# Attention softmax: the division by the row sums moved from the probabilities to the output of the product with V

## The chip, the core and the metric

One core of a Trainium2 chip runs the whole program. The metric is device time in microseconds of one execution; shorter is better. The engines are TensorE (PE, with its weight loads listed as PEld), VectorE (DVE), ScalarE (ACT), GpSimd (POOL), and the queue SP, which here issues all DMA transfers. Each engine works through its own queue in order.

## The reference

The program computes an attention block and two feed-forward blocks. Only the first part is touched here:

```python
B, H, S, D = q.shape                       # 4, 8, 576, 64
scores = scale * np.matmul(q, k.transpose(0, 1, 3, 2))
scores = np.where(causal, -1000000000.0, scores)
scores = scores - scores.max(-1, keepdims=True)
a = np.exp(scores)
a /= a.sum(-1, keepdims=True) + 1e-09
local = np.matmul(a, v)
...
return (g * mem_out + (1 - g) * local).astype(np.float32)
```

The result has 2304 tokens by 512 columns. It goes through `a*b @ w3 @ w_out` with `a = x @ w1`, `b = x @ w2`, and then through `(h - tanh h) @ w_out` with `h = x @ w_in`.

## The kernel before

The 32 heads are handled as 16 pairs P (two heads of one batch), and the 576 queries of a pair as five units u: u = 0 to 3 are 128 queries of each head, and u = 4 is the last 64 queries of both heads, stacked on 128 partitions. There are so 80 units. For each unit, `scores` makes the masked scores in PSUM (tile `sc`), `rmax` takes the negative row maximum on DVE into the small tile `st`, `exps` writes the exponentials to the tile `p` on ACT and lets the instruction add up the row sums into columns 2 and 3 of `st`, and `norm` makes the reciprocal of these sums on DVE (L416, L418, L420) and multiplies `p` by it on POOL, one instruction for each head (L427). `trans` turns `p` on PE, 128 by 128 blocks at a time, into the PSUM tile `t`, and `copy` brings `t` to the SBUF tiles `g`. `av` multiplies V with `g`, for units 0 and 1 as one group (256 queries) and for units 2 to 4 as another (320 queries), into the PSUM tile `o`, whose 128 partitions are the 64 columns of the two heads, and whose columns are the queries. The last step of `av` copies `o` to the tiles `xs`, scaled by `omgt`, which is 1 - g per partition.

`copy` shares its work: four of each five calls go to ACT (L438), the fifth to DVE (L440 or, with a scale, L442), counted over all its calls.

The loop over the units runs the steps in the order of `ORDER`, each with a lag:

```python
ORDER = "SENTLGA"
LAG = {'S': 0, 'E': 0, 'N': 0, 'T': 1, 'L': 0, 'G': 3, 'A': 2}
...
for m in range(NU + 8):
    for x in ORDER:
        do(x, m - LAG[x])
```

So `norm` of a unit stands one turn ahead of its `trans`, and `trans` one turn ahead of `av`. The letter L is one step of `prep_qk` for the next pair: it splits q and k in two parts each, on ACT, POOL and DVE (L204, L208, L219, L224, L226), and at its end issues the load of the pair after (`r`, one buffer). The letter G runs some steps of background work: decoding of the weights (L74 to L99, on ACT, DVE and POOL), the product of w3 and w_out (PSUM tile `fo`, which shares its two buffers with `o`), and the memory term. The order in each engine's queue isn't that of the program text: the framework simulates a timeline with its own costs and sorts the instructions by it, within their dependences (`schedule_with_timeline_sim=True`).

The PSUM pools are `pss` with four buffers (`sc`), `psT` with two (`t`) and `psA` with two (`o`). After the attention, phase B makes the first feed-forward block and phase C the second.

Of the kernel before, what the change touches and what calls it, by code (L numbers as in the profile page):

```python
# [11 lines left out]
F32 = mybir.dt.float32  # L12
F32R = mybir.dt.float32r
BF16 = mybir.dt.bfloat16
U32 = mybir.dt.uint32
U16 = mybir.dt.uint16
I64 = mybir.dt.int64
AF = mybir.ActivationFunctionType
# [6 lines left out]

# (h - tanh h) / h^3 as a product of two squares plus constants in u = h^2, for u <= TANH_SPLIT^2
TANH_SPLIT = 0.6
# [5 lines left out]
def block_kernel(ctx, tc, qk, qt, vt, mp, zp_d, beta, w1, w2, w3t, wo, wi, wo2, ident_d, mask_d, out):  # L33
# [11 lines left out]

# [1 line left out]
    ident = cp.tile([128, 128], F32, name="ident")  # L47
# [11 lines left out]

# [1 line left out]
    def dec_load(src):  # L61
# [39 lines left out]
    class Decoder:  # L101
        """Decodes a list of (source, destination) in turn, some at a time, with its loads ahead."""

# [38 lines left out]
    def mm(o, lhsT, rhs, start, stop):  # L142
        return PE.matmul(o, lhsT, rhs, start=start, stop=stop).ins  # L143
# [31 lines left out]
    CPA = (0, 1, 3, 4)  # L175
# [1 line left out]
    att = ExitStack()  # L177
# [9 lines left out]
    KH, KL = [[[t[:, x, h] for h in range(2)] for t in KF] for x in range(2)]  # L187
    V = [ap1.tile([128, 5, 2, 64], F32, name=f"v{i}") for i in range(2)]

    raw_t = {}  # L190
# [41 lines left out]

# [1 line left out]
    WF = {}  # L234
# [66 lines left out]
    if True:  # L301
# [23 lines left out]
        for i in range(2):  # L325
            PO.memset(QF[i][:, 0:64].bitcast(U32), 0)
            PO.memset(QF[i][:, 1216:1280].bitcast(U32), 0)
        xs = {}

# [11 lines left out]

# [1 line left out]
        pst = ExitStack()  # L343
# [40 lines left out]
        def rmax(n, x):  # L384
# [11 lines left out]
            if u == 4 and x == 1:  # L396
                DV.tensor_tensor(out=st_t[n][:, 0:1], in0=st_t[n][:, 0:1], in1=st_t[n][:, 1:2], op=ALU.min)

        def exps(n, x):
            P, u = units[n]  # L400
            st = st_t[n]
            if x == 0:
                p_t[n] = ap3.tile([128, PW[u]], F32, tag=f"p{u}" if PU else "p", name="p")
            w = width(u, x)
            o = x * (w if u < 4 else 320)
            b = x if u < 4 else 0
            mark["A"][n] = AC.activation(out=p_t[n][:, o:o + w], in_=sc_t.pop((n, x))[:, 0:w], func=AF.Exp,  # L407
                                         bias=st[:, b:b + 1], accum_out=st[:, 2 + x:3 + x]).ins

        def norm(n):  # L410
            P, u = units[n]
            hp = P % 4
            st, p = st_t.pop(n), p_t[n]
            w = 2 if u < 4 else 1
            if u < 4:
                DV.tensor_scalar(out=st[:, 4:6], in0=st[:, 2:4], scalar1=1e-9, scalar2=None, op0=ALU.add)  # L416
            else:
                DV.scalar_tensor_tensor(out=st[:, 4:5], in0=st[:, 2:3], scalar=1e-9, in1=st[:, 3:4],  # L418
                                        op0=ALU.add, op1=ALU.add)
            DV.reciprocal(out=st[:, 6:6 + w], in_=st[:, 4:4 + w])  # L420
            K = 128 * (u + 1) if u < 4 else 576
            for h in range(w):
                pr, sc = p[:, K * h:K * h + K], st[:, 6 + h:7 + h]
                if NV[u] == "A" or NV[u] == "H" and h or NV[u] == "Q" and P % 2:
                    AC.activation(out=pr, in_=pr, func=AF.Copy, scale=sc)
                else:
                    (DV if NV[u] == "V" else PO).tensor_scalar(out=pr, in0=pr, scalar1=sc, scalar2=1.0, op0=ALU.mult, op1=ALU.mult)  # L427

# [15 lines left out]
        def trans(n):  # L444
            P, u = units[n]
            p = p_t.pop(n)
            if u == 0:
                g_t[0] = ap2.tile([128, 2, 2, 256], F32, tag="g0", name="g0")
            if u == 2:
                g_t[1] = (ap1, ap2)[G1 - 1].tile([128, 4, 2, 320], F32, tag="g1", name="g1")  # L450
                g_t[2] = ap2.tile([64, 2, 64], F32, tag="g2", name="g2")
            if u < 4:
                K = 128 * u + 128
                blocks = [(kb, h) for kb in range(u + 1) for h in range(2)]
                for c in range(0, len(blocks), 4):
                    ch = blocks[c:c + 4]
                    t = psT.tile([128, 4, 128], F32, tag="t", name="t")
                    for m, (kb, h) in enumerate(ch):
                        PE.transpose(t[:, m], p[:, K * h + 128 * kb:K * h + 128 * kb + 128], ident)  # L459
                    G = g_t[0] if u < 2 else g_t[1]  # L460
                    q0 = 128 * (u % 2)
                    copy(G[:].rearrange("p a b q -> p (a b) q")[:, c:c + len(ch), q0:q0 + 128], t[:, 0:len(ch)])
            else:
                t = psT.tile([128, 4, 128], F32, tag="t", name="t")
                for kb in range(4):
                    PE.transpose(t[:, kb], p[:, 128 * kb:128 * kb + 128], ident)
                copy(g_t[1][:].rearrange("p a b q -> p (a b) q")[:, :, 256:320],
                     t[:].rearrange("p a (b q) -> p (a b) q", b=2))
                t = psT.tile([128, 4, 128], F32, tag="t", name="t")
                PE.transpose(t[0:64, 0], p[:, 512:576], ident)  # L470
                copy(g_t[2][:], t[0:64, 0].rearrange("p (b q) -> p b q", b=2))

        finished = [0]

        def av(P, grp):
# [5 lines left out]
            if grp == 0:  # L481
                for kb in range(2):
                    for h, r in hr:
                        mm(o[r, 128 * kb:256], v[:, kb, h], g_t[0][:, kb, h, 128 * kb:256], kb == 0, kb == 1)
            else:
                for kb in range(4):
                    q0 = 128 if kb == 3 else 0
                    for h, r in hr:
                        mm(o[r, q0:320], v[:, kb, h], g_t[1][:, kb, h, q0:320], kb == 0, False)
                for h, r in hr:  # L490
                    mm(o[r, 256:320], v[0:64, 4, h], g_t[2][:, h], False, True)
            ch = b * 9 + grp * 4
            finished[0] = 2 * P + grp + 1
            for X, e0, e1, s in xpart(ch, ch + n // 64):
                copy(X[:, e0:e1, hp], o[:, 64 * s:64 * (s + e1 - e0)].rearrange("p (a b) -> p a b", b=64),
                     omgt[:, hp:hp + 1])

# [1 line left out]
        N = 384  # L499
# [139 lines left out]
        def do(x, n):  # L639
# [15 lines left out]
            elif x == "T":  # L655
                trans(n)
            elif x == "A" and u in (1, 4):
                av(P, u // 4)
# [26 lines left out]

# [1 line left out]
        pools = {}  # L687
# [169 lines left out]

# [1 line left out]
        c2 = ctx.enter_context(tc.tile_pool(name="c2", bufs=2))  # L859
# [180 lines left out]
```

## Time and profile before

| | |
|---|---|
| median of 3 runs | 1068.35 us (1066.63 to 1069.19) |
| span of the profiled execution | 1064.0 us |
| mean granted TensorE clock | 0.973 |
| PE busy | 991.2 us, 93% of the span |
| DVE busy | 824.1 us, 77% |
| ACT busy | 609.3 us, 57% |
| POOL busy | 439.8 us, 41% |

The span runs from the first to the last instruction of the profiled execution. Its own time isn't listed apart from that; the median of the runs is 4.35 us above the span. Busy time is the union of an engine's instructions. Matmuls are pipelined, so that PE can be called busy while it could still take more work. The product with V of the last pair, the end of the attention, stands at some 305 us; phase B and C follow.

### The profile page before, as it was taken

To read this page: it belongs to the slowest core of one execution; us is meant where nothing else is said; L and a number is where in the kernel's file an instruction comes from. 1 tells how busy PE (TensorE), PEld (TensorE's weight loads), DVE (VectorE), ACT (ScalarE), POOL (GpSimd) and SP (SyncE) were. 2 spreads that over 40 slices of the span, in tenths; PEclk is the share of its full clock that TensorE was granted. 3 is DMA by queue.
4 is the path that set the end of the run, shared out by engine and by line. 5 is a ranking of instruction groups with operands and counts; after the bars stand their busy time and mean duration, and the time that the engine had idled before them with its cause. 6 is when DMAs were issued, how large, how long until landed. Compare 5 with 4: busy or idle time off the path is not lost.

```text
span 1064.0 us, 15807 instructions
## 1 busy us (share of the span) xinstructions
PE 991.2 (93%) x5512; PEld 863.2 (81%) x5512; DVE 824.1 (77%) x1465; ACT 609.3 (57%) x1413; POOL 439.8 (41%) x446
## 2 busy tenths in 40 slices
PE   5889898976999899999999997999999999999998
PEld 3566666654688798999999987789999999999997
DVE  7999999999869985557221498988878787787875
ACT  5767677666832332324121444678777776776864
POOL 5788677777655432200000485532222222222221
PEclk8899999999999999999999998999999999999999
DMA  7665575554324451123100013000000000000000
GB/s 199 162 161 153 165 190 132 140 136 124 94 74 131 157 155 60 50 70 130 50 1 1 20 60 99 20 1 30 1 1 30 1 30 1 1 31 2 30 1 30
DMA packets 44415, 77.73 MB, mean 73 GB/s; under 512 B 5168, under 2 KB 30000, under 8 KB 42416
## 3 DMA queue, kind: packets, MB, share of 16 engines
q1 hardware_dynamic: 44336, 76.73, 25.3%
q8 instruction: 43, 0.70, 0.3%
q14 instruction: 36, 0.29, 0.1%
HBM read 72.00 MB, written 4.72 MB: 72 GB/s over the span
## 4 chain that ended last, share of the span: by engine, by line
PE 61%; DVE 18%; DMA 8%; POOL 6%; issue 4%; ACT 2%; SPq 0%; DVEq 0%; POOLq 0%; ACTq 0%
PE o L143 20%; PE h L143 18%; PE ab L143 13%; PE x L143 6%; DMA r<-in_qk 6%; DVE T L81 2%; DVE T L75 2%; DVE T L84 2%; POOL p L427 1%; DMA raw<-in_wo 1%; DVE T L77 1%; DVE qs L224 1%; PE mo L143 1%; DVE st L394 1%; PE t L459 1%
## 5 line engine op out<-in xcount | busy, mean ns | idle before, releaser
L922 POOL TENSOR_TENSOR gl<-s,gh 128x384 fp32r<-128x384 f32 x96 | 102.2, 1065 | 285.2 <-ACT gh L916 266.8
L427 POOL TENSOR_SCALAR p<-p,st 128x128 f32<-128x128 f32 (+2 forms) x144 | 111.4, 787 | 45.0 <-DVE st L420 25.3
L143 PE MATMUL ab<-xh,wa 128*128 128x384 f32 x384 | 110.1, 344 | 4.9 <-DVE a L723 1.9
L143 PE MATMUL x<-abh,wf 128*128 128x384 f32 x384 | 109.3, 346 | 3.2 <-ACT abh L726 3.2
L143 PE MATMUL ab<-xh,wb 128*128 128x384 f32 x384 | 108.3, 340 | 3.5 <-POOL wb L96 3.1
L143 PE MATMUL sc<-ks,qs 128*128 128x256 f32 (+4 forms) x384 | 91.3, 355 | 14.4 <-DVE qs L224 8.8
L898 DVE SCALAR_TENSOR_TENSOR s<-s,u 128x384 f32<-128x384 f32 x96 | 82.6, 860 | 24.3 <-ACT s L888 23.5
L407 ACT ACTIVATE p<-sc,st 128x256 f32<-128x256 f32 (+4 forms) x160 | 82.6, 524 | 28.4 <-DVE st L391 11.7
L74 ACT ACTIVATE T<-raw 128x512 f32<-128x512 f32 x72 | 48.5, 674 | 86.8 <-DMA raw<-in_wo 29.0
L723 DVE TENSOR_TENSOR a<-ab,a 128x384 f32<-128x384 f32 x48 | 26.5, 552 | 81.2 <-PE ab L143 68.5
L894 ACT ACTIVATE u<-u,pc 128x384 f32<-128x384 f32 x96 | 59.3, 619 | 43.9 <-DVE s L898 43.8
L143 PEld LDWEIGHTS ab<-xh,wa 128*128 128x128 f32 x384 | 71.1, 190 | 9.7 <-issue 3.3
L143 PEld LDWEIGHTS sc<-ks,qs 128*128 128x128 f32 x384 | 62.2, 203 | 20.3 <-ACT ks L204 7.5
L143 PEld LDWEIGHTS x<-abh,wf 128*128 128x128 f32 x384 | 71.9, 192 | 4.4 <-ACT abh L726 4.1
L904 DVE TENSOR_TENSOR t<-h,t 128x384 f32<-128x384 f32 x96 | 53.2, 554 | 28.5 <-ACT t L887 28.0
L143 PEld LDWEIGHTS ab<-xh,wb 128*128 128x128 f32 x384 | 71.0, 190 | 4.8 <-POOL wb L96 3.8
L459 PE MATMUL t<-ident,p 128*128 128x128 f32 x320 | 53.0, 286 | 20.2 <-ACT g L438 8.1
L903 DVE SCALAR_TENSOR_TENSOR s<-s,s 128x384 f32<-128x384 f32 x96 | 65.5, 682 | 7.9
L143 PE MATMUL x<-abl,wf 128*128 128x384 f32 x192 | 66.3, 345 | 3.8 <-DVE abl L727 3.7
L886 ACT ACTIVATE u<-h 128x384 f32<-128x384 f32 x96 | 46.9, 488 | 39.8 <-PE h L143 39.8
L143 PE MATMUL h<-xh,wf 128*128 128x384 f32 x240 | 67.7, 343 | 1.0 <-DVE s L905 1.0
L143 PE MATMUL h<-xh,z 128*128 128x384 f32 x240 | 66.7, 338 | 0.8 <-DVE s L905 0.8
(205 smaller groups left out, 2811.9 us busy)
## 6 DMA issues: line engine op xcount, KB each, us to landing
r<-in_qk SPq DMA_DIRECT2D x30, 576.0 KB, 6.7
raw<-in_wo SPq DMA_DIRECT2D x24, 512.0 KB, 3.5
raw<-in_w3t SPq DMA_DIRECT2D x16, 512.0 KB, 4.6
raw<-in_w SPq DMA_DIRECT2D x16, 512.0 KB, 3.6
raw<-in_wi SPq DMA_DIRECT2D x16, 512.0 KB, 3.7
v<-in_vt SPq DMA_DIRECT2D x16, 320.0 KB, 5.1
mw<-in_qt SPq DMA_DIRECT2D x18, 256.0 KB, 3.0
out<-ob SPq DMA_DIRECT2D x18, 256.0 KB, 2.3
```

What stands on the lines that cost most here:

```text
L74: AC.activation(out=tf, in_=hw.bitcast(F32), func=AF.Abs)
L143: return PE.matmul(o, lhsT, rhs, start=start, stop=stop).ins
L407: mark["A"][n] = AC.activation(out=p_t[n][:, o:o + w], in_=sc_t.pop((n, x))[:, 0:w], func=AF.Exp, bias=st[:, b:b + 1], accum_out=st[:, 2 + ...
L427: (DV if NV[u] == "V" else PO).tensor_scalar(out=pr, in0=pr, scalar1=sc, scalar2=1.0, op0=ALU.mult, op1=ALU.mult)
L459: PE.transpose(t[:, m], p[:, K * h + 128 * kb:K * h + 128 * kb + 128], ident)
L723: DV.tensor_tensor(out=a, in0=o[1][:, 0:N], in1=a, op=ALU.mult)
L886: AC.activation(out=u, in_=o, func=AF.Square)
L894: AC.activation(out=u, in_=u, func=AF.Relu, bias=pc[:, 2:3])
L898: DV.scalar_tensor_tensor(out=s1, in0=s1, scalar=k2[0], in1=u, op0=ALU.add, op1=ALU.mult)
L903: DV.scalar_tensor_tensor(out=s1, in0=s2, scalar=k2[1], in1=s1, op0=ALU.add, op1=ALU.mult)
L904: DV.tensor_tensor(out=t, in0=o, in1=t, op=ALU.subtract)
L922: PO.tensor_tensor(out=l, in0=s1, in1=h[:].bitcast(F32), op=ALU.subtract)
```

## The change

`exps` lets the sums of all units of a group go to one tile `sg`. `norm` does nothing for units 0, 2 and 3; at units 1 and 4, the last of their groups, it adds 1e-9 and takes the reciprocals of the whole group at once on DVE, and lets POOL spread the first four columns of them into a tile `rb` of 128 by 256, each column 64 times. The tile `p` isn't multiplied any more: `trans` reads what `exps` wrote. A new step `spread`, behind `trans` of the same unit, turns `rb` on PE with two transposes, and for the second group a fifth column with a third, into a tile of the pool `psT`; ACT then copies this to a tile `rr` and multiplies by `omgt` on the way, in one instruction for the first group and in three for the second. The last step of `av` is now a DVE multiplication of `o` by `rr`, instead of the copy with a scale; it doesn't count any more for the share-out in `copy`. The tile `g2`, of 64 partitions before, has 128, whose upper half is set to zero at the start; the last two matmuls of a group multiply with all 128 rows of it.

```diff
+    G2 = [ap1.tile([128, 2, 64], F32, name=f"g2{i}") for i in range(2)]
...
+            PO.memset(G2[i][64:128].bitcast(U32), 0)
...
+        sum_t, rr_t, inv_t = {}, {}, {}
+
         def exps(n, x):
             P, u = units[n]
             st = st_t[n]
+            grp, a = (0, 2 * u) if u < 2 else (1, 2 * u - 4)
+            if u in (0, 2) and x == 0:
+                sum_t[P, grp] = ap4.tile([128, 16], F32, tag="sg", name="sg")
+            sg = sum_t[P, grp]
...
-                                         bias=st[:, b:b + 1], accum_out=st[:, 2 + x:3 + x]).ins
+                                         bias=st[:, b:b + 1], accum_out=sg[:, a + x:a + x + 1]).ins
 
         def norm(n):
             P, u = units[n]
-            hp = P % 4
-            st, p = st_t.pop(n), p_t[n]
-            w = 2 if u < 4 else 1
-            if u < 4:
-                DV.tensor_scalar(out=st[:, 4:6], in0=st[:, 2:4], scalar1=1e-9, scalar2=None, op0=ALU.add)
-            else:
-                DV.scalar_tensor_tensor(out=st[:, 4:5], in0=st[:, 2:3], scalar=1e-9, in1=st[:, 3:4],
+            st_t.pop(n)
+            if u not in (1, 4):
+                return
+            grp = u // 4
+            sg = sum_t.pop((P, grp))
+            DV.tensor_scalar(out=sg[:, 8:12], in0=sg[:, 0:4], scalar1=1e-9, scalar2=None, op0=ALU.add)
+            if grp:
+                DV.scalar_tensor_tensor(out=sg[:, 12:13], in0=sg[:, 4:5], scalar=1e-9, in1=sg[:, 5:6],
                                         op0=ALU.add, op1=ALU.add)
-            DV.reciprocal(out=st[:, 6:6 + w], in_=st[:, 4:4 + w])
-            K = 128 * (u + 1) if u < 4 else 576
-            for h in range(w):
-                pr, sc = p[:, K * h:K * h + K], st[:, 6 + h:7 + h]
-                if NV[u] == "A" or NV[u] == "H" and h or NV[u] == "Q" and P % 2:
-                    AC.activation(out=pr, in_=pr, func=AF.Copy, scale=sc)
-                else:
-                    (DV if NV[u] == "V" else PO).tensor_scalar(out=pr, in0=pr, scalar1=sc, scalar2=1.0, op0=ALU.mult, op1=ALU.mult)
+            w = 13 if grp else 12
+            DV.reciprocal(out=sg[:, 8:w], in_=sg[:, 8:w])
+            rb = ap2.tile([128, 256], F32, tag="rb", name="rb")
+            PO.tensor_scalar(out=rb[:].rearrange("p (a b) -> p a b", b=64),
+                             in0=sg[:, 8:12].unsqueeze(2).to_broadcast([128, 4, 64]),
+                             scalar1=1.0, scalar2=1.0, op0=ALU.mult, op1=ALU.mult)
+            inv_t[P, grp] = sg, rb
+
+        def spread(n):
+            P, u = units[n]
+            if u not in (1, 4):
+                return
+            grp, hp = u // 4, P % 4
+            sg, rb = inv_t.pop((P, grp))
+            t = psT.tile([128, 4, 128], F32, tag="t", name="rt")
+            for m in range(2):
+                PE.transpose(t[:, m], rb[:, 128 * m:128 * m + 128], ident)
+            if grp:
+                PE.transpose(t[:, 2], sg[:, 12:13].to_broadcast([128, 128]), ident)
+            r = rr_t[P, grp] = ap2.tile([128, 320], F32, tag="rr", name="rr")
+            o = omgt[:, hp:hp + 1]
+            AC.activation(out=r[:, 0:256], in_=t[:, 0:2].rearrange("p a b -> p (a b)"), func=AF.Copy, scale=o)
+            if grp:
+                for h in range(2):
+                    x = slice(64 * h, 64 * h + 64)
+                    AC.activation(out=r[x, 256:320], in_=t[x, 2, x], func=AF.Copy, scale=o[x])
...
-                g_t[2] = ap2.tile([64, 2, 64], F32, tag="g2", name="g2")
+                g_t[2] = G2[P % 2]
...
-                copy(g_t[2][:], t[0:64, 0].rearrange("p (b q) -> p b q", b=2))
+                copy(g_t[2][0:64], t[0:64, 0].rearrange("p (b q) -> p b q", b=2))
...
-                    mm(o[r, 256:320], v[0:64, 4, h], g_t[2][:, h], False, True)
+                    mm(o[r, 256:320], v[:, 4, h], g_t[2][:, h], False, True)
...
+            rr = rr_t.pop((P, grp))
             for X, e0, e1, s in xpart(ch, ch + n // 64):
-                copy(X[:, e0:e1, hp], o[:, 64 * s:64 * (s + e1 - e0)].rearrange("p (a b) -> p a b", b=64),
-                     omgt[:, hp:hp + 1])
+                c = slice(64 * s, 64 * (s + e1 - e0))
+                DV.tensor_tensor(out=X[:, e0:e1, hp], in0=o[:, c].rearrange("p (a b) -> p a b", b=64),
+                                 in1=rr[:, c].rearrange("p (a b) -> p a b", b=64), op=ALU.mult)
...
                 trans(n)
+                spread(n)
```

## Rows read from the trace of the kernel before

**Rows 1.** Busy time in stretches: start:end, length, then each engine, clock, DMA.
```profile
0.00:100.00 100.00, 79.06 (x447) 56.71 (x447) 88.49 (x171) 64.89 (x177) 75.14 (x90) 0.90 0.66 170
100.00:250.00 150.00, 129.32 (x847) 94.40 (x849) 143.82 (x286) 100.24 (x284) 111.34 (x124) 0.97 0.57 151
250.00:305.00 55.00, 49.02 (x342) 33.83 (x339) 43.80 (x110) 36.19 (x103) 34.57 (x43) 0.97 0.31 88
305.00:450.00 145.00, 134.12 (x766) 123.14 (x765) 114.03 (x215) 49.52 (x105) 57.14 (x48) 0.96 0.36 111
```

**Rows 2.** Waits, DVE, 0 to 305 us: total us, times, longest.
```profile
DVE ks L226 <- POOL ks L208: 4.2, 6, 1.7
...
DVE g L440 <- PE t L466: 1.3, 1, 1.3
```

**Rows 3.** Groups by line, DVE, 0 to 305 us: busy, mean ns, idle before.
```profile
L224 DVE SCALAR_TENSOR_TENSOR qs<-r,qs 64x576 fp32r<-64x576 f32 x32 | 31.3, 990 | 7.5 <-ACT qs L219 6.6
...
L226 DVE TENSOR_TENSOR ks<-r,ks 128x576 fp32r<-128x576 f32 x16 | 21.7, 1353 | 4.2 <-POOL ks L208 4.2
L416 DVE TENSOR_SCALAR st<-st 128x2 f32<-128x2 f32 x64 | 19.6, 307 | 0.1
L75 DVE TENSOR_SCALAR T<-T 128x512 f32<-128x512 f32 x30 | 19.1, 636 | 3.2 <-ACT T L74 2.8
L77 DVE TENSOR_SCALAR T<-T 128x512 uint32<-128x512 uint32 x30 | 18.6, 619 | 0.2
L440 DVE COPY g<-t 128x512 f32<-128x512 f32 (+2 forms) x29 | 17.6, 609 | 1.3 <-PE t L466 1.3
...
L420 DVE RECIPROCAL st<-st 128x2 f32<-128x2 f32 (+1 forms) x80 | 11.9, 155 | 0.3
L418 DVE SCALAR_TENSOR_TENSOR st<-st 128x1 f32<-128x1 f32 x16 | 10.9, 682 | 1.1 <-ACT p L407 1.1
...
L587 DVE TENSOR_TENSOR xs<-mo,xs 128x384 f32<-128x384 f32 x4 | 2.2, 554 | 0.4 <-PE mo L143 0.4
```

**Rows 4.** Instructions of tile xs, 0 to 305 us: shortest/median/longest ns, first and last start.
```profile
L442 DVE TENSOR_SCALAR xs<-o,omgt x4: 339/440/539, 43.7 to 267.6; 128x192 f32<-128x192 f32 x1, 128x128 f32<-128x128 f32 x1, 128x256 f32<-128x256 f32 x1, 128x320 f32<-128x320 f32 x1
```

**Rows 5.** Groups by line, POOL, 0 to 305 us.
```profile
L427 POOL TENSOR_SCALAR p<-p,st 128x128 f32<-128x128 f32 (+2 forms) x144 | 111.4, 787 | 45.0 <-DVE st L420 25.3 <-DVE st L416 9.9 <-PE sc L143 3.0
...
L99 POOL TENSOR_TENSOR zs<-T,zs 128x512 fp32r<-128x512 f32 x16 | 22.4, 1400 | 1.3
```

**Rows 6.** Groups by line and shape, POOL, 0 to 305 us.
```profile
L427 POOL TENSOR_SCALAR p<-p,st 128x256 f32<-128x256 f32 x32 | 21.4, 680 | 12.1 <-DVE st L416 7.1 <-PE sc L143 3.0 <-DVE st L420 1.5
```

**Rows 7.** Instructions of four DVE lines, 0 to 305 us: shortest/median/longest ns.
```profile
L75 DVE TENSOR_SCALAR T<-T x30: 409/430/1516, 13.3 to 265.6; 128x512 f32<-128x512 f32 x30
...
L77 DVE TENSOR_SCALAR T<-T x30: 405/427/1422, 14.2 to 268.8; 128x512 uint32<-128x512 uint32 x30
...
L224 DVE SCALAR_TENSOR_TENSOR qs<-r,qs x32: 749/783/1880, 6.6 to 264.6; 64x576 fp32r<-64x576 f32 x32
...
L226 DVE TENSOR_TENSOR ks<-r,ks x16: 745/1332/1986, 7.4 to 260.4; 128x576 fp32r<-128x576 f32 x16
```

**Rows 8.** Timeline: start, length, engine, line, count: eight transposes in a row.
```profile
197.65 1.04 PE L459 MATMUL t<-ident,p 128*128 128x128 f32 x8
```

**Rows 9.** Waits, PE, 0 to 305 us: total us, times, longest.
```profile
PE t L459 <- ACT g L438: 8.1, 8, 3.0
PE fo L143 <- POOL zs L96: 7.9, 5, 2.4
PE t L459 <- DVE g L440: 6.4, 8, 1.5
...
PE t L459 <- POOL p L427: 4.6, 3, 2.3
```

**Rows 10.** Groups by line and shape, ACT, 0 to 305 us.
```profile
L219 ACT ACTIVATE qs<-r 128x576 fp32r<-128x576 f32 x32 | 21.0, 680 | 16.3 <-DMA r<-in_qk 16.3
...
L438 ACT ACTIVATE g<-t 128x256 f32<-128x256 f32 x29 | 11.2, 386 | 5.4 <-PE t L459 5.4
...
L438 ACT ACTIVATE xs<-o,omgt 128x256 f32<-128x256 f32 x15 | 7.1, 472 | 2.0 <-PE o L143 2.0
...
L438 ACT ACTIVATE g<-t 64x128 f32<-64x128 f32 x13 | 3.4, 260 | 0.3 <-PE t L470 0.3
```

## The prediction

> **What bounds the kernel now.** I began with busy time in stretches [rows 1]. The attention ends at some 305 us, and everything that the change touches lies ahead of that. In its middle, 100 to 250 us, DVE is busy for 143.8 of 150 us (96%), PE for 129.3, ACT for 100.2, POOL for 111.3. So DVE sets the pace there. At both ends it is less clear: in the other 155 us of the attention DVE is busy for 88.5 + 43.8 = 132.3, or 85%. Over all 305 us the sums are DVE 276.1, PE 257.4 and POOL 221.1. What comes behind 305 us is untouched, and there PE is busy for 134.1 of the first 145 us: a shorter attention starts that part earlier, and changes nothing in it.
>
> The second view is who waits for whom. DVE hardly waits: 4.2 us for POOL's part of k, 1.3 us in all for transposed blocks, though it fetches some thirty of them from PE [rows 2]. PE waits more: 14.5 us in 16 pieces for `t` to be emptied, 7.9 us for weights that POOL splits and 4.6 us for the scaled `p` [rows 9]. ACT's largest single wait is 16.3 us for the load of q and k [rows 10].
>
> The third view is the duration of one DVE instruction. Lines whose operands all lie in SBUF scatter: L75 takes 409 ns at the shortest and 636 in the mean, L77 405 and 619, L224 749 and 990, L226 745 and 1353 [rows 3, 7]. The multiplication L587, with one input in PSUM, is at 554 [rows 3]. So something in SBUF holds DVE up, and POOL, busy for 72% of this stretch, is the engine that I hold it to be. Half of POOL's time is L427, 111.4 of 221.1 us [rows 1, 5], and just this goes.
>
> **DVE's own work.** Removed: 64 additions at 307 ns (19.6 us), 16 of L418 at 682 (10.9), 80 reciprocals at 155 (12.4) [rows 3], and four copies to `xs` at 440 (1.8) [rows 4]: 44.7 us. Added: with one set for each of 32 groups, 32 additions (9.8), 16 of L418 (10.9), 32 reciprocals (5.0), all at the same durations, since widths of 1 to 5 columns differ in nothing that counts. Then the multiplications of `o` by `rr`. There are 36: 16 of 256 columns, 12 of 320, and 4 pairs whose group is cut at token block 6, in 128 and 192. The copies L442 do the same move in 339 ns at 128 columns and 539 at 320, thus 1.04 ns a column [rows 4]; by them the 36 cost 17.0 us. L587 takes 554 for 384 columns with two inputs of the same kinds [rows 3]; with the same slope 256 cost 421, 320 cost 487, and the 36 cost 15.1. I take 15.1, the same operation, and keep 17.0 as the upper end. Added are 40.8 us, 3.9 less than removed. Since these steps leave the count in `copy`, a fifth of 138 calls (128 of `t`, 10 of the memory term) stays with DVE, about 28; now it has 29 and one more that isn't shown; two fewer at 609 are 1.2 us [rows 3]. DVE's own work falls by 5.1 us.
>
> **What POOL gives back to DVE.** The four scattering lines lose 30 x 227 + 30 x 214 + 32 x 241 + 16 x 608 ns = 30.6 us against their shortest [rows 3, 7]. POOL loses 111.4 us of L427 and gains 32 spreads of 256 columns; nearest is L427 at that width, 680 ns, so 21.8 us [rows 5, 6]. POOL's time falls by 89.6 of 221.1 us, 40%, and 40% of 30.6 is 12.2 us. The bounds are 0 (if POOL's longer instructions, L99 at 1400 ns and its like, do the holding [rows 5]) and 27 (if nearly all of it is L427, which stands close behind DVE's small steps). L427 is short at 787 ns in the mean, which speaks for less than its share; L81, L84 and L397, of the same kind and left out of the sum, for more. I stay at 12.2. DVE in all: -17.3 us.
>
> A rule of the Trainium skill (SBUF — State Buffer, Who interferes with whom) says that GpSimd and a VectorE instruction with two SBUF inputs, or in a mode that uses both ports, exclude each other for a whole instruction, the later one being blocked fully. By that rule every overlap that goes is time for one of the two, and the gain would lie near the upper bound; no row here divides the blocked time between them.
>
> **PE.** It gets 2 transposes for each of 32 groups and a third for 16: 80. Eight in a row take 1.04 us [rows 8], so at most 0.13 us each, 10.4 us in all. PE's 257.4 us become 268, while DVE's 276.1 become 259. PE would pass DVE if its shown time were full; it is not, since matmuls overlap and the shown time holds the tail of each run. I cost the 10.4 us at nothing, under DVE's work, and let only half of the gain pass where DVE isn't full; uncovered they are 10 us. The last two matmuls of a group multiply 128 rows in place of 64, with the same columns: nothing, under the same cover, as is the zeroing at the start, on an idle POOL.
>
> On this point the Trainium skill (TensorE: Matmul & The Clock Gate, Part 4: PE-mode transpose) speaks against the change: it gives a transpose some 275 ns in a kernel, which as a cost would be an estimated 22 us for the 80. The trace doesn't agree to that as a cost, since eight take 1.04 us, 0.13 each [rows 8].
>
> **ACT and the waits.** ACT loses 32 copies to `xs` of about 472 ns (15 us) and gains 32 of 256 columns at 386 (12.4) and 32 of 64 by 64, at most 260 each (8.3) [rows 10]: up 6 us, on an engine with 104 us free (305 less 201 busy, [rows 1]); nothing. No DMA is moved; the loads of `r` are set free by L224 and L226, which come sooner if DVE is quicker. POOL's spread waits for DVE's reciprocal, with POOL's splits behind it; PE's transposes of `rb` wait for it, with the next scores behind them. Both stand a turn ahead of the product with V, and the multiplication by `rr` is the only wait at the end. There DVE waits for `o`, with the row maxima and so the exponentials behind it. By the 1.3 us over 29 copies [rows 2, 3] that is 0.045 us each, 1.6 us for 36.
>
> **Sum.** From 100 to 250 us DVE is at 96%, so its share of the gain passes through: 17.3 x 150/305 = 8.5 us. In the remainder, with DVE at 85% and the load of `r` waited for [rows 1, 10], I let half pass: 4.4. Less 1.6 for the new wait makes 11.3 us. The span goes from 1064.0 to 1052.7; the median stands 4.35 us above the span, so 1068.35 becomes 1057.0.
>
> **Rivals.** *POOL was the real brake.* L427 also holds the splits that PE waits for (7.9 us) and `p` itself (4.6) [rows 9], and the DVE steps that stay could fall toward their undisturbed length. With 27 us of relief, DVE's work falls by 32; with the waits on POOL gone too, some 27 us pass: 1041. For it: POOL is busy for 74% in the middle stretch. Against: PE, at 86% there, is next [rows 1].
>
> *The tile `rt` blocks PE (slower).* It is a third use of the two buffers of `psT` right behind the two of unit 4, so PE stands until ACT or DVE has emptied the first, with the scores of the next units behind. PE now waits 14.5 us over 133 emptied tiles, 0.11 us each, but a wait that occurs is 0.9 us (14.5/16) and up to 3.0 [rows 9]. With 0.11 for each of 32 new tiles nothing happens (3.5 us). At 1.5 us each it is 48 us: PE needs 257.4 + 10.4 + 48 = 316 us, 11 us more than the 305 now: 1079. It decides from about 0.5 us a tile: 305 - 268 leaves 37, of which some 20 stay with waits for POOL and ACT (7.9 + 4.6 + 8.1, [rows 9]). For it: the planner orders by its own costs, which needn't match the chip's. Against: it can put scores between.
>
> *Nothing comes through.* PE's 10.4 us and a few waits use up just what DVE gives: 1067, within 0.2% (2 us), about what a measurement of this kernel tells from no change.
>
> **Chances.** Forecast 0.45 (own range 1050 to 1063), POOL as the brake 0.17, nothing 0.12, the blocked PE 0.26. So faster 0.62, same 0.12, slower 0.26. The range runs from the first rival's 1041 to the second's 1079, cut at 1078; outside stays the farther part of each, some 0.2.
>
> **What would show it.** Right: attention ending near 294 us; L75, L77, L224 and L226 shorter in the mean by a third of their excess; POOL busy near 130 us until then; DVE still over 90% in the middle. Wrong: PE waiting on `t` for over 20 us more, DVE waiting for `o` by more than some us, or DVE's lines as long as before.

## The result and the profile after

The changed kernel takes 1079.49 us (median of 4 runs, 1077.07 to 1081.79) against 1067.63 before (the 1068.35 above is the median of three runs, this one of four): a ratio of 1.0101, 95% interval 1.0074 to 1.0128. It is 12 us slower, where 11 faster was forecast. The time lies just above the range, near the 1079 of the second rival.

First the page's line of busy times, for the kernel after:

```profile
PE 1002.7 (93%) x5592; PEld 870.3 (81%) x5592; DVE 807.3 (75%) x1414; ACT 619.3 (58%) x1448; POOL 348.5 (32%) x336
```

Then busy time in stretches, with columns as in [rows 1]:

```profile
0.00:100.00 100.00, 74.31 (x415) 53.73 (x416) 78.72 (x147) 58.07 (x161) 42.77 (x56) 0.90 0.66 169
100.00:250.00 150.00, 134.14 (x881) 96.93 (x879) 134.63 (x261) 107.62 (x306) 65.08 (x68) 0.99 0.56 145
250.00:305.00 55.00, 49.71 (x335) 33.38 (x337) 38.68 (x91) 40.04 (x122) 13.25 (x17) 0.91 0.36 99
305.00:450.00 145.00, 134.20 (x780) 120.40 (x778) 118.32 (x219) 52.91 (x112) 60.24 (x49) 0.98 0.36 111
```

DVE is less busy in the middle, 134.6 us where it was 143.8, and POOL 65.1 where it was 111.3 [rows 1]. But PE went from 129.3 to 134.1. The last product with V starts at 317.5 us; it started at 304.4. The row of the whole attention up to that start, before:

```profile
0.00:304.40 304.40, 256.80 (x1630) 184.41 (x1632) 276.11 (x565) 201.02 (x563) 220.87 (x254) 0.94 0.56 146
```

and after:

```profile
0.00:317.50 317.50, 270.66 (x1709) 193.44 (x1711) 260.75 (x514) 210.88 (x600) 125.93 (x144) 0.95 0.54 140
```

DVE lost 15.4 us of work and POOL 95. PE gained 13.9, and its idle time (length less busy) is 47.6 before and 46.8 after: the attention is 13.1 us longer, about what PE has more. The granted TensorE clock, a mean over stretches at its two levels of 2.4 and 1.2 GHz, is 0.94 of the higher one before and 0.95 after in these two rows, so it isn't what made the attention longer. What DVE saved it now waits: its idle time went from 28.3 to 56.7 us. Its waits up to 318 us (total, times, longest), beside [rows 2]:

```profile
DVE st L396 <- PE sc L143: 9.3, 11, 2.4
DVE ks L227 <- POOL ks L209: 8.2, 5, 3.5
...
DVE g L467 <- PE t L486: 5.3, 6, 2.7
DVE s L295 <- PE fo L143: 4.7, 4, 2.5
...
DVE xs L524 <- PE o L143: 2.9, 4, 2.0
```

The four rows on PE come to 22.2 us; for transposed blocks it was 1.3, now 5.3. The groups of DVE, same stretch (busy, mean ns, idle before), beside [rows 3]:

```profile
L225 DVE SCALAR_TENSOR_TENSOR qs<-r,qs 64x576 fp32r<-64x576 f32 x32 | 31.0, 986 | 7.4 <-ACT qs L220 6.7
L84 DVE SCALAR_TENSOR_TENSOR T<-raw,T 128x512 uint32<-128x512 uint32 x30 | 30.6, 1022 | 0.2
...
L227 DVE TENSOR_TENSOR ks<-r,ks 128x576 fp32r<-128x576 f32 x16 | 17.5, 1093 | 8.3 <-POOL ks L209 8.2
...
L77 DVE TENSOR_SCALAR T<-T 128x512 uint32<-128x512 uint32 x30 | 14.7, 490 | 0.3
L524 DVE TENSOR_TENSOR xs<-o,rr 128x256 f32<-128x256 f32 (+3 forms) x36 | 14.7, 414 | 2.9 <-PE o L143 2.9
L75 DVE TENSOR_SCALAR T<-T 128x512 f32<-128x512 f32 x30 | 14.6, 485 | 2.4 <-ACT T L74 2.2
...
L425 DVE TENSOR_SCALAR sg<-sg 128x4 f32<-128x4 f32 x32 | 9.0, 280 | 1.0 <-ACT p L415 0.7
...
L430 DVE RECIPROCAL sg<-sg 128x4 f32<-128x4 f32 (+1 forms) x32 | 5.6, 177 | 0.4
...
L427 DVE SCALAR_TENSOR_TENSOR sg<-sg 128x1 f32<-128x1 f32 x16 | 3.1, 191 | 1.6 <-ACT p L415 1.4
```

The groups of PE that hold the new transposes, with what PE waited for ahead of them:

```profile
L445 PE MATMUL rt<-ident,rb 128*128 128x128 f32 x64 | 13.3, 291 | 6.3 <-ACT g L465 4.1 <-POOL z L96 1.1 <-DVE g L467 0.9
...
L447 PE MATMUL rt<-ident,sg 128*128 128x128 f32 x16 | 4.6, 290 | 0.0
```

and ACT's new copies:

```profile
L450 ACT ACTIVATE rr<-rt,omgt 128x256 f32<-128x256 f32 x32 | 15.5, 484 | 4.2 <-PE rt L445 2.2 <-PE rt L447 1.9
...
L454 ACT ACTIVATE rr<-rt,omgt 64x64 f32<-64x64 f32 x32 | 10.0, 312 | 0.2
```

### The profile page after: what moved, and what is told of

It is laid out like the page before. It is cut to its first block, busy times and chain, and to the rows that moved or that the text cites. A ratio compares the mean times of both kernels' runs of the same rounds, so it can differ in the third digit from the quotient of the medians.

```text
span 1075.1 us, 15801 instructions
## 1 busy us (share of the span) xinstructions
PE 1002.7 (93%) x5592; PEld 870.3 (81%) x5592; DVE 807.3 (75%) x1414; ACT 619.3 (58%) x1448; POOL 348.5 (32%) x336
## 3 DMA queue, kind: packets, MB, share of 16 engines
q1 hardware_dynamic: 44336, 76.73, 25.5%
## 4 chain that ended last, share of the span: by engine, by line
PE 56%; DVE 4%; POOL 2%; issue 1%; ACT 1%; DMA 0%; DVEq 0%; SPq 0%; POOLq 0%
PE o L143 18%; PE h L143 18%; PE ab L143 12%; PE x L143 6%; PE mo L143 1%; DVE T L75 1%; DVE T L81 1%; POOL wa L816 0%; DVE abl L757 0%; DVE T L77 0%; POOL gl L952 0%; DVE T L84 0%; POOL wb L816 0%; PE mo L599 0%; DMA mw<-in_qt 0%
## 5 line engine op out<-in xcount | busy, mean ns | idle before, releaser
L143 PEld LDWEIGHTS sc<-ks,qs 128*128 128x128 f32 x384 | 62.2, 204 | 24.1 <-ACT p L415 10.6
L465 ACT ACTIVATE g<-t 128x512 f32<-128x512 f32 (+2 forms) x102 | 50.3, 508 | 27.8 <-PE t L486 24.0
```

What stands on the lines that cost most here:

```text
L465: AC.activation(out=dst, in_=src, func=AF.Copy, scale=1.0 if scale is None else scale)
```

## The experiments

The main theory after the result (A): PE's queue sets the attention's length, and the 80 transposes lengthen it. The rivals: (B) with the multiplication gone, the planner finds a worse order; (C) the multiplication on DVE waits for PE and holds `o`; (D) DVE sets the length, as predicted; (E) the new copies load ACT and hold `psT`; (F) PE waits for the chain of reciprocal and spread; (G) the additional claims on `psT`'s two buffers cost, not the work in them; (H) the place of the transposes in PE's queue.

Eighteen kernels were run. The table gives each one's median less that of the kernel before on the same chip, the ratio with its interval, and, from its profile, the attention up to the start of the last product with V: length, PE busy, PE idle (the difference) and DVE busy, in us. The ratio isn't simply the quotient of the two medians; the two differ most for after_copy, where 1.0035 is 3.7 us and the medians differ by 1.6. The lengths come from one profiled execution each.

| kernel | us | ratio | length | PE busy | PE idle | DVE busy |
|---|---|---|---|---|---|---|
| before | | | 304.4 | 256.8 | 47.6 | 276.1 |
| changed | +11.9 | 1.0101 (1.0074 to 1.0128) | 317.5 | 270.7 | 46.8 | 260.8 |
| pe80 | +6.9 | 1.0070 (1.0055 to 1.0085) | 315.1 | 270.3 | 44.8 | 280.1 |
| dve_add | +6.8 | 1.0069 (1.0049 to 1.0089) | 314.7 | 260.2 | 54.5 | 282.5 |
| no_mult | -5.9 | 0.9951 (0.9932 to 0.9969) | 299.1 | 254.7 | 44.4 | 258.1 |
| rr_const | -9.1 | 0.9914 (0.9896 to 0.9931) | 295.8 | 253.9 | 41.9 | 261.0 |
| rr_const_bg | -3.6 | 0.9968 (0.9953 to 0.9983) | 302.3 | 256.7 | 45.6 | 262.5 |
| neither | -4.9 | 0.9951 (0.9934 to 0.9968) | 300.3 | 255.9 | 44.4 | 252.9 |
| after_copy | +1.6 | 1.0035 (1.0017 to 1.0053) | 305.9 | 267.3 | 38.6 | 250.2 |
| rt_noread | +6.5 | 1.0060 (1.0040 to 1.0079) | 313.9 | 268.1 | 45.8 | 261.7 |
| rt_ident | +8.1 | 1.0075 (1.0055 to 1.0096) | 316.1 | 267.8 | 48.3 | 264.4 |
| claim_only | +5.8 | 1.0051 (1.0031 to 1.0070) | 314.1 | 266.4 | 47.7 | 262.7 |
| work_only | +4.8 | 1.0039 (1.0024 to 1.0055) | 311.8 | 265.3 | 46.5 | 259.5 |
| rt_shared | +1.8 | 1.0018 (1.0002 to 1.0034) | 312.3 | 266.8 | 45.5 | 260.5 |
| rt_shared2 | +7.7 | 1.0071 (1.0051 to 1.0092) | 315.2 | 265.3 | 49.9 | 263.3 |
| rt_shared2_pp | +2.1 | 1.0019 (1.0005 to 1.0034) | 307.8 | 261.5 | 46.3 | 261.0 |
| rt_shared_pp | +3.2 | 1.0026 (1.0013 to 1.0039) | 310.7 | 268.6 | 42.1 | 262.7 |
| before_bg | -2.4 | 0.9983 (0.9970 to 0.9997) | 304.4 | 258.4 | 46.0 | 271.2 |
| after_bg | +18.0 | 1.0155 (1.0129 to 1.0182) | 329.4 | 277.7 | 51.7 | 261.9 |
| spread_late | +21.1 | 1.0199 (1.0174 to 1.0224) | 329.2 | 275.0 | 54.2 | 264.6 |

**pe80**: the 80 transposes with their 32 tiles of `psT`, in the kernel before.

```diff
             elif x == "T":
                 trans(n)
+                if u in (1, 4):
+                    t = psT.tile([128, 4, 128], F32, tag="t", name="rt")
+                    for k in range(2 + u // 4):
+                        PE.transpose(t[:, k], ident, ident)
```

> The kernel before, with the 80 additional transposes of the change and nothing else of it: at units 1 and 4, behind trans, two or three transposes of the identity into a tile of psT that nothing reads. Theory A (PE's queue sets the attention's length, so that work added to PE counts in full): slower by 9 to 14 us, most of the change's loss of 12. Theory B (with the multiplication gone the planner sorts the queues otherwise, and the engines wait for one another more): within 3 us of before. Theory C (the multiplication of the output on DVE, which waits for PE and holds the tile o): within 3 us of before.

It was 6.9 us slower, so what was added isn't hidden, though less than the full A. As the tiles are claimed too, the run doesn't tell A from G. Its row of the attention shows PE at 270.3, 13.5 us more for 32 visits, 0.42 us a visit:

```profile
0.00:315.10 315.10, 270.34 (x1721) 195.86 (x1721) 280.08 (x567) 200.97 (x565) 220.96 (x254) 0.95 0.54 141
```

**no_mult**: POOL's multiplication left out of the kernel before, by a `break` ahead of it.

> The kernel before without the multiplication of p on POOL (L427), all else as it was; the division by the row sums is left out of the result. Theory A: PE's work is as before, so within 3 us of before, or faster by up to 5 for the waits on p. Theory B: slower by 6 to 12 us, although it only leaves work out. Theory C, and the prediction's own sum: faster by 8 to 15 us.

5.9 us faster. DVE lost 18.0 us (276.1 to 258.1) without an instruction of its own being taken, so the relief is real, and at most a third of it came through, since PE's waits for `p` (4.6 us, [rows 9]) went too. That is less than C and the prediction's own sum asked for (8 to 15). B's forecast falls: taking the multiplication out didn't make a bad order here.

**dve_add**: the mirror of pe80, work on DVE alone.

```diff
                 copy(X[:, e0:e1, hp], ...)
+                DV.tensor_reduce(out=RO, in_=RC[:, 0:64 * (e1 - e0)], axis=AX.X, op=ALU.max)
```

> The kernel before with one more DVE instruction behind each copy to xs: a maximum over 128 to 320 columns of a constant tile in SBUF, 36 in all, some 15 us of DVE work that nothing waits for. Theory A (PE's queue sets the attention's length): slower by at most 5 us. Theory D (the prediction's: DVE, 96% busy in the middle, sets it): slower by 10 to 15 us.

6.8 us slower, between the theories. The group of the added instructions in this kernel:

```profile
L500 DVE TENSOR_REDUCE ro<-rc 128x1 f32<-128x256 f32 (+3 forms) x36 | 14.8, 412 | 1.7 <-POOL rc L327 1.3
L77 DVE TENSOR_SCALAR T<-T 128x512 uint32<-128x512 uint32 x30 | 14.5, 482 | 0.1
```

Of 14.8 us of added instructions 6.8 us, 46%, passed. But DVE's busy time rose by 6.4 us only, as other lines got shorter in the new order, L77 from 619 ns [rows 3] to 482; so the share that passes is known only roughly. DVE counts, but it isn't the bound by itself; nor, by pe80, is PE.

**rr_const**: the changed kernel without the transposes, `rt` and the copies.

```diff
-            t = psT.tile([128, 4, 128], F32, tag="t", name="rt")
-            ... (transposes and copies)
+            rr_t[P, grp] = RC
```

> The changed kernel without the transposes, the tile rt and ACT's copies to rr: the output is multiplied by a constant tile, so the division by the sums and the gate are left out of the result. Reciprocals and POOL's spread stay. Theory A: the loss is gone, within 3 us of before or faster by some us. Theory B: most of the loss stays, slower than before by 6 to 12 us. Theory C: most of the loss stays too.

9.1 us faster than before, 21.0 faster than the changed kernel: the whole loss goes with these steps, taken together. The row of the attention:

```profile
0.00:295.80 295.80, 253.87 (x1644) 185.52 (x1644) 260.95 (x517) 192.63 (x539) 135.23 (x145) 0.96 0.58 151
```

DVE's work is that of the changed kernel, 261; PE has 16.8 us less.

**after_copy** has the last step of `av` as before, and **neither** has that and no transposes.

```diff
-                DV.tensor_tensor(out=X[:, e0:e1, hp], in0=o[:, c]..., in1=rr[:, c]..., op=ALU.mult)
+                copy(X[:, e0:e1, hp], o[:, c].rearrange("p (a b) -> p a b", b=64), omgt[:, hp:hp + 1])
```

> The changed kernel with the last step of av as it was before: copy with the scale omgt, shared between ACT and DVE; rr is computed and not read, so the division is left out of the result. Theory A: as the changed kernel, slower than before by 9 to 14 us. Theory B: the same. Theory C: within 3 us of before or faster.

> The changed kernel without the transposes and ACT's copies, and with the last step of av as it was before (copy with omgt); sums, reciprocals and POOL's spread as in the change, the division left out of the result. It fills the fourth place beside the changed kernel (+11.9 us), the one without transposes (-9.1) and the one with the old last step (+1.6). If the costs of the transposes and of the multiplication add up: faster than before by 17 to 20 us. If each only costs where the other is there: faster by 8 to 12.

With transposes the old step is 10 us better by the medians (+1.6 against +11.9) and 7 by the ratios, as C said; without them it is 4 us worse (-4.9 against -9.1). Neither forecast of the second text came. C isn't shown by this: the old step also takes 10.6 us off DVE (260.8 to 250.2), and each of the four kernels is one order (see Order below).

**rt_noread** (transposes, no copies out of `rt`) and **rt_ident** (the same, with the identity as input).

```diff
-                PE.transpose(t[:, m], rb[:, 128 * m:128 * m + 128], ident)
+                PE.transpose(t[:, m], ident, ident)
```

> The changed kernel with the transposes of rb into rt, but without ACT's copies out of it; the output is multiplied by a constant tile, so the division is left out of the result. Without both it was faster than before by 9.1 us, with both slower by 11.9. Theory A (PE's own time for the 80 transposes): slower than the kernel without both by 8 to 13 us, so within 4 us of before. Theory E (the buffer of psT is held until ACT, which works in order, has read it, and ACT has more to do): at most 4 us slower than the kernel without both, so faster than before by 5 to 9.

> The changed kernel with the same 80 transposes into rt, but of the identity, so that they wait for no reciprocal and no spread; no copies out of rt, the output multiplied by a constant tile, so the division is left out of the result. The same with rb as input was 6.4 us slower than before, without transposes it was 9.1 faster. Theory A (PE's own time, the buffer of psT): again slower than before by 3 to 7 us. Theory F (PE stands still until the chain of reciprocal and spread has come through): faster than before by 2 to 6.

The transposes with their tiles take rr_const from -9.1 to +6.5, and to +8.1 if they wait for no reciprocal. E and F fall: neither ACT's copies nor the chain of reciprocal and spread carry the loss, at most the last 5 us of it.

**rt_shared** moves the second group's transposes into free columns of a tile that unit 4 claims anyway.

```diff
                 PE.transpose(t[0:64, 0], p[:, 512:576], ident)
+                sg, rb = inv_t[P, 1]
+                for m in range(2):
+                    PE.transpose(t[:, 1 + m], rb[:, 128 * m:128 * m + 128], ident)
+                PE.transpose(t[:, 3], sg[:, 12:13].to_broadcast([128, 128]), ident)
```

> The changed kernel with the three transposes of the second group put into the free three quarters of the second tile of unit 4, so that 16 of the 32 additional claims on the two buffers of psT go; same result as the changed kernel, which is 11.9 us slower than before. Theory A (PE's own time): within 3 us of the changed kernel. Theory G (the claims on psT, the rival of the prediction): some 4 to 8 us faster than the changed kernel, so 4 to 8 slower than before.

Ten of the twelve us came back (nine by the ratios), with all the work still there. In its profile the attention got only 5.2 us shorter, 317.5 to 312.3, so the size isn't firm. **claim_only** and **work_only** were to part claims from work, both on rr_const: the one claims a tile 32 times for a single transpose of 64 by 64, the other puts 80 transposes into free quarters of tiles of units 2 and 4.

> The changed kernel without its 80 transposes and ACT's copies (output multiplied by a constant tile, so the division is left out; that was 9.1 us faster than before), but with the 32 additional claims on the buffers of psT kept: each claims a tile and puts a single transpose of 64 by 64 into it. Theory G (the claims cost): loses 8 us or more against the kernel without, so about before or slower. Theory A (PE's time for the transposes costs): loses at most 4, so 5 to 9 faster than before.

> The same kernel without transposes and copies, but with the 80 transposes of 128 by 128 put (of the identity) into the free quarters of tiles that psT gives out anyway, two in the second tile of unit 2 and three in the second of unit 4: PE's work without any additional claim; the division is left out. Theory G: loses at most 4 us against the kernel without, so 5 to 9 faster than before. Theory A: loses 8 us or more, so about before or slower.

Each loses against rr_const nearly what both lose together (15.6 in rt_noread): 14.9 and 13.9 us. In claim_only the mechanism of the second rival is there to see; PE's waits (total, times, longest):

```profile
PE rt L447 <- ACT g L458: 15.1, 5, 6.3
...
PE rt L447 <- DVE g L460: 1.4, 2, 0.9
```

16.5 us ahead of the claimed tiles, up to 6.3 at a time. In work_only there is no such claim, and PE is 11.4 us busier. But claim_only isn't free of work either. Its row of the attention, two of its groups of PE, and the first of these in rr_const:

```profile
0.00:314.10 314.10, 266.37 (x1657) 189.42 (x1659) 262.66 (x513) 191.65 (x536) 128.73 (x145) 0.92 0.55 142
```

```profile
L143 PE MATMUL o<-g,v 128*64 128x320 f32 x192 | 38.8, 553 | 0.3 <-DVE g L460 0.3
...
L447 PE MATMUL rt<-ident 64*64 64x64 f32 x32 | 8.0, 251 | 16.6 <-ACT g L458 15.1 <-DVE g L460 1.4
```

```profile
L143 PE MATMUL o<-g,v 128*64 128x320 f32 x192 | 34.4, 493 | 2.2 <-DVE g L458 2.2
```

PE is 12.5 us busier than in rr_const, more than in work_only, and its idle time is only 5.8 us longer (47.7 against 41.9): the waits ahead of `rt` came mostly in place of others. One small transpose costs PE 0.25 us a visit, 8.0 in all. The same 192 products with V take 4.4 us more, beside a lower granted clock, 0.92 over the attention where rr_const has 0.96. A stretch of claim_only shows how; first two windows of 4 us, then PE's timeline in them:

```profile
264.00:268.00 4.00, 0.71 (x5) 0.52 (x5) 3.58 (x5) 3.44 (x7) 2.18 (x2) 1.00 0.53 161
268.00:272.00 4.00, 4.00 (x20) 2.69 (x20) 3.60 (x10) 2.32 (x9) 0.32 (x1) 0.50 0.20 54
```

```profile
266.92 0.30 PE L490 MATMUL t<-ident,p 128*64 128x128 f32 x1 [3.33 <-ACT g L458]
...
270.17 4.11 PE L143 MATMUL o<-g,v 128*64 128x320 f32 x16
```

and, in the changed kernel:

```profile
157.97 2.16 PE L143 MATMUL o<-g,v 128*64 128x320 f32 x16
```

PE waits 3.3 us for a tile of `psT`, and from 268 to 272 us the clock is at its lower level, 1.2 GHz (0.50); 16 products with V take 4.11 us there, where the changed kernel makes 16 of them in 2.16 at the higher level. So PE's busy time holds some of its waits' cost, and the two runs don't part claims from work: in both PE gets 11 to 13 us busier, and the losses don't add.

**rt_shared2** moves the first group's transposes too, into unit 2's second tile; **rt_shared2_pp** and **rt_shared_pp** also set `KLE` to "PP", so that POOL makes both subtractions of k.

> The changed kernel, complete and with the same result, with all transposes of reciprocals in free quarters of other tiles: the second group's in the second tile of unit 4 (which alone took it from 11.9 to 1.8 us slower than before), the first group's two in the second tile of unit 2. No additional claim on psT is left. Theory G: another 5 to 10 us, so 3 to 8 faster than before. Theory A: no further gain, within 3 us of the kernel with one group moved.

> The kernel of the run before, and with both subtractions of prep_qk's k on POOL, which the change has set free, in place of one on DVE and one on POOL: some 17 us off DVE, 25 onto POOL. If DVE's load counts by some 0.3 to 0.45, as in the runs so far: 5 to 8 us faster than without. If PE alone sets the length: within 2 us of it.

> The changed kernel with the second group's transposes in the second tile of unit 4 (1.8 us slower than before), and with both subtractions of k on POOL, which made 5.6 us in the kernel with all transposes moved. If DVE's load counts here as there: 2 to 6 us faster than before, and the first complete version ahead of both kernels. If the order decides: anywhere from 5 faster to 8 slower.

Without any additional claim it is 7.7 us slower, worse than with one group moved: G's second forecast falls. The edit has a cost of its own, though: the first group's transposes come a unit later, and the last step of `av` now waits for `rr`, 2.2 us in all, which it doesn't in the changed kernel. POOL's help made 5.6 us in the one and nothing in the other (+1.8 to +3.2).

**Order.** **before_bg**, **after_bg** and **rr_const_bg** have `BG` at 2.10, not 2.13; **spread_late** issues `spread` just ahead of `av`.

> The kernel before with the background pace 2.10 in place of 2.13 steps a unit, which changes no work and only the order that the planner finds. If the order in itself is worth little: within 2 us of before. If a new order alone can move the time as much as the change did: off by 4 us or more.

> The changed kernel with the background pace 2.10 in place of 2.13, no work changed and the order found anew, as was done with the kernel before, which came out 1.8 us faster by it. If the order is worth little: within 3 us of the changed kernel. If the loss is an accident of one order: 5 us or more faster than it.

> The changed kernel without transposes and ACT's copies (output multiplied by a constant tile, the division left out), at the background pace 2.10 in place of 2.13: the order found anew. At 2.13 it was 9 us faster than before; the whole change was 12 slower at 2.13 and 17 slower at 2.10. If the 9 us are the gain that all the rest of the change brings: 6 to 12 us faster than before. If they were one good order: within 4 us of before.

> The changed kernel with the step spread issued a turn later, right ahead of the product with V of its group, in place of right behind the transposes of its last unit; same work, same result. Theory A: within 3 us of the changed kernel. Theory F or H (the place in PE's queue: the transposes of rb stand ahead of others that are ready): 4 us or more faster than the changed kernel.

With the same work the kernel before moves by 2.4 us, rr_const by 5.5, the changed one by 6.1 and, with `spread` later, by 9.2 (slower, where F and H wanted it faster). So differences under some 6 us between two kernels here can be the order's. The loss is no such accident: from rr_const to the changed kernel it is 21.0 us at 2.13 and 21.6 at 2.10, and from the kernel before to the changed one 11.9 and 20.4. What the rest of the change brings is less sure: 9.1 us at 2.13, but at 2.10, where the kernel before is faster too, 1.2 (-3.6 against -2.4). The second forecast for rr_const_bg came, that the 9 us were one good order; two orders put this gain anywhere from 1 to 9 us, and up to 5.5 us of what claim_only and work_only lost against rr_const may be that order too.

## Why the prediction was wrong

*The bound.* The step that failed stands at its start, that DVE, 96% busy in the middle, sets the pace, and in the sum, where PE's new work was costed at nothing under DVE's. The attention got longer by 13.1 us while DVE had 15.4 us less to do and PE 13.9 more. In the 20 profiles of the table DVE's busy time goes from 250 to 283 us, and the length hardly follows it (correlation 0.20, where 1 would be a straight line); it follows PE's busy time far more closely (0.91), with PE idle for 39 to 55 us, 47 in the mean. That is no law: in after_copy PE is 10.5 us busier than before, and the attention is 1.5 us longer. Both engines work in order and feed each other: instructions added to DVE passed at 46%, time taken off it at a third at most (no_mult), where I let 75% pass (12.9 of 17.3).

*PE's price.* 80 transposes were put at 10.4 us from a run of eight. PE got 13.9 us busier, as they come in 32 visits of two or three; in pe80 a visit is 0.42 us. That is the smaller error; the larger was to let none of it count.

*DVE's relief.* Right in the sum, partly by luck: 17.3 us less were forecast, 15.4 came, but from other places. The multiplications were put at 15.1 us and took 14.7. DVE's own steps were to fall by 3.9 us and fell by 11.8, from 44.2 (19.6 + 10.9 + 11.9 in [rows 3] and 1.8) to 32.4 (9.0 + 3.1 + 5.6 + 14.7): the kept ones got cheaper than assumed, L427 (L418 before) falling from 682 to 191 ns. The four lines that scatter lost 12.6 us of their excess over the shortest of before, against 12.2 forecast: from 30.6 us to 30 x 76 + 30 x 85 + 32 x 237 + 16 x 348 ns = 18.0. But the even 40% hides that L75 and L77 lost 60% or more of it, L226 43%, and L224, at 986 ns, almost nothing. And L84, left out of the sum, went from 779 to 1022 ns in the mean, 7 us over 30, and took back over half of that.

*The waits.* DVE's wait for `o` is 2.9 us, 1.6 forecast. ACT's copies took 25.5 us, 20.7 forecast, as a copy with its scale from a tile is the longer one in all these rows: 484 ns at 256 columns, as `xs` had 472, not 386 [rows 10]. The length of a transpose (the Trainium skill, TensorE: Matmul & The Clock Gate, Part 4: PE-mode transpose) gave an estimated 22 us for the 80. As a length the trace is near it, 291 and 290 ns in the rows above; PE's additional busy time, 13.9 us, lies between that estimate and my price.

*The rivals.* The second rival's time is what came, 1079, but not as it was put: PE waits 6.3 us ahead of `rt`, not 48, and no more in all than before. Its mechanism is seen in claim_only, and rt_shared's 10 us fit it, but no run holds it apart from PE's work and from the order. The first rival, POOL as the brake, has no support beyond no_mult's 6 us. Of the signs set down, POOL's 126 us and the shorter lines came as for "right", and no sign was set for what happened: PE busier at the same idle time.

*Open.* How the 21 us divide between the work of the transposes, the claims on `psT` and the multiplication on DVE. Each of three edits, taking away the claims of one group, the old last step, or all transposes, returns 10 us or more by the medians (7 or more by the ratios), and they don't add. As a new order alone moves the changed kernel by 6 to 9 us, the 10 us of rt_shared and of after_copy don't prove a mechanism by themselves; the 21 us, found at two paces, do show where the loss sits: in the transposes, their tiles and the copies together. Fixing the queue order by hand, so that only one of these changes, wasn't tried. No complete version with the change is ahead of the kernel before. The only complete one that is ahead of both is before_bg, at 0.9983.

## What to carry to other kernels

When two engines that work in order are both over 85% busy and feed each other, don't call a cost on one of them hidden by the other: here about half of what was added to either came through (dve_add, pe80), and at most a third of what was taken from one. Price short visits on PE by the visit, not by the piece of a long run, and count each new claim on a PSUM pool of two buffers as a possible wait for whoever empties it. Where a planner sorts the queues, draw the order of both kernels once more with no work changed before reading a difference of half a per cent, and compare at the same setting.

## What the hardware showed unexpectedly

The single-column instruction L418 in no_mult, in before_bg, and L84 in the kernel before:

```profile
L418 DVE SCALAR_TENSOR_TENSOR st<-st 128x1 f32<-128x1 f32 x16 | 4.4, 276 | 1.3 <-ACT p L407 1.1
L418 DVE SCALAR_TENSOR_TENSOR st<-st 128x1 f32<-128x1 f32 x16 | 7.0, 439 | 1.2 <-ACT p L407 1.1
L84 DVE SCALAR_TENSOR_TENSOR T<-raw,T 128x512 uint32<-128x512 uint32 x30 | 23.4, 779 | 0.1
```

A DVE instruction on a single column (L418) took 682 ns in the mean before, 276 in no_mult, where only the multiplication on POOL is left out, and 191 after; so that work on POOL lengthened it. How much depends on the order: in before_bg, with the multiplication in place, it takes 439. L84 went up from 779 to 1022 ns in the mean, though POOL is busy for 126 us in place of 221, and is at 855 in after_bg with the same work: POOL's total alone doesn't decide how long a line takes, and the order of the queues counts too. An ACT copy with its scale read from a tile takes about 0.1 us more than one with a constant (484 and 472 ns against 386 at 256 columns). And a wait of PE can cost twice: behind one of 3.3 us in claim_only the clock was at 1.2 GHz, and 16 products with V took 4.11 us in place of 2.16.
